# Split first units, paired slot sums, and two output rows computed ahead of the last sum, in a gated recurrence followed by a soft mixture of experts

## The chip, the cores and the metric

The kernel runs on one core of a Trainium2 chip. The core has five engines with a queue each: TensorE (PE, matmuls and transposes through matmul, results in PSUM), VectorE (DVE), ScalarE (ACT), GpSimd (POOL) and SyncE (SP, which here only issues DMAs). POOL issues the weight loads, and 16 DMA engines carry all transfers. The metric is device time in microseconds (us) of one execution; 0.5% of it is about 1 us.

## The reference

```python
# x, f_logit: (4, 5056, 256); phi: (256, 32); w1: (8, 256, 1024); w2: (8, 1024, 256)
sig = 1.0 / (1.0 + np.exp(-f_logit))
f = lower_bound + (1.0 - lower_bound) * sig
i = 1.0 - f
for t in range(S):
    h = f[:, t] * h + i[:, t] * x[:, t]
    y[:, t] = h
x = y.reshape(B * S, D)                      # 20224 tokens
logits = x @ phi                             # 32 slots, 4 per expert
d = softmax(logits over tokens)              # per slot
slot_input = d.T @ x                         # 32 x 256
slot_out[e] = relu(slot_input[e] @ w1[e]) @ w2[e]
c = softmax(logits over slots)               # per token
return c @ slot_out
```

A recurrence over 5056 tokens in four batches is followed by two softmaxes over the same logits: one over all tokens, which gathers 32 slot inputs, and one over the slots, which spreads the experts' results back over the tokens. No output row can be finished before all tokens have been read.

## The kernel before, in words

A unit is 512 tokens of one batch (`G = 128 * R`, `R = 4`); there are 10 groups of tokens (`n_grp`) and 4 batches, so 40 units (`n_unit`). `place(n)` says which group and batch unit n is. Two units with numbers 2m and 2m+1 share the tiles of a load. The order of the instructions on every engine is the order in which the program writes them (`manual_schedule`).

For a unit the steps are: `load` (SP issues the DMAs of `f_logit` and `x` into `f_t`, `x_t`, three buffers each); `gate` (ACT, line 234: `s_t` = sigmoid(-f), for two units at once, for one in units 0 to 3); `enter` (POOL, line 245: `u_t` = s * x; DVE for unit 0); `s_to_channels` and `u_to_channels` (PE transposes into PSUM tiles `sp`, `up`, lines 249, 257, 264: tokens on partitions become channels on partitions); `decay` (ACT, lines 297, 304: a = 1 - (1-lb) s); `scan` (DVE, lines 319, 332: the recurrence, two instructions per unit, carrying on from the previous group of the batch); `to_tokens` (PE, line 345: transposes back into `hp`) and `keep_tokens` (line 364: copy into `ht`, by ACT or DVE). After four units of a group: `logits` (PE, line 378), `exps` (ACT, line 387: exp into `etall`, which stays in SBUF for all tokens), `weights_to_tokens` (PE transposes, line 399, and a copy, line 402), and `slots` (PE, line 428), which adds exp(logits).T @ h of a group to one PSUM tile `slot_ps`, 32 rows per batch:

```python
for b in range(B):
    nc.tensor.matmul(slot_ps[ds(b * NS, NS), :], et[:n_p, r, b], ht[:n_p, b, r], ...)
```

`idle(k)` (line 183) issues fp32 matmuls that no result needs. `W_AT` says after which unit's `enter` POOL issues the next weight load (`load_w`); 16 loads of 512 KB in SBUF (1 MB in memory, cast on the way), the last one, the second matrix of expert 7, in chunks of 4, 2 and 2 of its 8 slices (line 147, into `w_sb` and `w_t`).

The loop over the units writes, in iteration n, the loads of unit n+6, the gate of n+3 or n+4, the enter of n+3, transposes of units n+1 to n+3, the scan of n, and copies and sums of earlier units. After it come the last group's sums, the copy of the slot sums to `slot_sb` (line 615), four matmuls that sum the batches into `sin_ps` (line 619, a corner of the tile `tail`, in which PE also writes row sums of `etall` at line 411), the scaling into `sin` (631, 632), the first expert matrices (line 648) with relu (653, 655), transposes (663), the second matrices of experts 0 to 3 (684) and of experts 4 to 7 (line 696, into `so_ps`, after which `spin` issues eight matmuls, line 152), the scaling by the reciprocal `rcs` of the softmax sum into `slot_out` (DVE, line 708), and two copies of it with rows of every other batch zeroed, `slot_bd` (POOL, line 710).

The output is then computed in blocks of rows: `share` (line 727) multiplies `etall` of 128 tokens by `slot_out` of a batch; `by_vector` (DVE, 717) and `by_scalar` (ACT, 721, 767) scale by `rrow`, the reciprocal of the row sums; SP issues the DMAs to memory. The first are `pieces(0, 0)`: block 0 (2048 tokens, 16 rows a partition) of batch 0 in five DMAs of 2, 2, 2, 4 and 6 rows (line 749); then `by_rows` of the last block, two batches at once through `slot_bd` (lines 760, 770); then `rest`, `whole` (789) and `couple` (801 to 815).

Of the kernel before, what the change touches and what calls it, by code (L numbers as in the profile page):

```python
# [18 lines left out]
def kernel(  # L19
# [62 lines left out]
    nc.vector.tensor_copy(ident, ident_f)  # L82

# [78 lines left out]
    with tc.tile_pool(name="sp2", bufs=3) as sp2, \  # L162
# [10 lines left out]
        slot_ps = slot_bank[:, 0]  # L173
# [3 lines left out]
        def idle(k, first=False):  # L177
            if first:
                for i in range(2):
                    nc.tensor.matmul(slot_bank[:, 1, ds(0, P)], ident, ident,  # L180
                                     start=True, stop=False, skip_group_check=True)
            for _ in range(k):
                nc.tensor.matmul(slot_bank[:, 1], ident_f, wide_rep,  # L183
                                 start=False, stop=False, skip_group_check=True)
# [75 lines left out]
        def half_to_channels(n, ps, t):  # L260
            k = ds(n % 2 * (P // 2), P // 2)
            v = ps.rearrange("c p r -> c (p r)").rearrange("c (p r) -> c p r", r=2 * R)
            for r in range(2 * R):
                nc.tensor.transpose(v[:, :, r], t(r)[k].bitcast(F32), ident_f[k, k])  # L264
# [10 lines left out]
        def u_to_channels(n):  # L275
            ps = psu.tile([P, P, R], F32, name="up", tag="up")
            if long(n):
                half_to_channels(n, ps, lambda r: uts[n - n % 2 + r // R][:, r % R])
# [143 lines left out]

        def slots(g):
            n_p = rows(g)
            et, ht = ets.pop(g), hts.pop(g)
            for r in range(R):
                for b in range(B):
                    nc.tensor.matmul(slot_ps[ds(b * NS, NS), :], et[:n_p, r, b],
                                     ht[:n_p, b, r],
                                     start=(g == 0 and r == 0),  # L430
                                     stop=(g == n_grp - 1 and r == R - 1),
                                     skip_group_check=True)
# [37 lines left out]
        def late_slots():  # L470
            for r in range(R):
                for b in range(B):
                    nc.tensor.matmul(slot_ps[ds(b * NS, NS), :], ets[last][:, r, b],
# [10 lines left out]
        lb_constants()  # L484
        gate(0, 1)
# [3 lines left out]
        u_to_channels(0)  # L489
        gate(1, 1)  # L490
# [3 lines left out]
        s_to_channels(1)  # L494
        u_to_channels(1)
# [3 lines left out]
        for n in range(n_unit):  # L499
            if n < SINGLE - 2:  # L500
# [7 lines left out]
                if n + 3 == SINGLE:  # L508
                    gate(n + 3)
                if n % 2 == 0:  # L510
                    unit(load, n + AHEAD)
                unit(enter, n + 3)
                for b in range(2 * n, 2 * n + 2):
                    rep_constants(b)
            else:
# [31 lines left out]
                if n == n_unit - 2:  # L547
                    keep_tokens(n - 1)
                if n % 2 == 0:
# [320 lines left out]
```

## Time and profile before

| what | value |
|---|---|
| time before, median of 3 runs | 197.21 us (196.96 to 197.81) |
| the profiled execution's own time | 197.01 us |
| its span, first to last instruction | 195.2 us |
| mean granted TensorE clock | 0.845 |
| busy: PE, DVE, ACT, POOL | 150.6, 142.0, 138.8, 103.1 us |
| moved by DMA | 70.75 MB; HBM read 58.23 MB, written 20.71 MB |

The page divides the span into 40 slices of 4.88 us and gives for each the busy share of an engine in tenths (9 is 90% or more), the clock that TensorE was granted and the busy share of the 16 DMA engines. The chain that ended last is followed back from the last instruction: at each step to what released it. A line of the timeline has the start, the length, the engine, the line of the kernel, the operation, the tiles written and read, the shape, the count, and in brackets how long the engine was idle before and what ended that. A line of the table of stretches has the stretch, its length, the busy time and number of instructions of each engine, the granted clock, the DMA share and GB/s. Loads of weights count in GB/s with what is written to SBUF, half of what is read, as they are cast.

### The profile page before, as it was taken

The numbers are of one execution on the slowest core, as the hardware profiler recorded it, in microseconds if no ns is written. First come the engines' busy times: TensorE is split into PE (matmuls) and PEld (weight loads), VectorE is DVE, ScalarE is ACT, GpSimd is POOL, SyncE is SP. The second block draws the span as 40 slices with busy tenths as digits, with TensorE's granted clock in tenths as the row PEclk, the third lists the DMA queues.
The fourth block names the chain that finished last, engine by engine and source line by source line (L and its number), as shares of the span: only waits on it lengthen the run. The fifth ranks groups of instructions, "written<-read, shape, count | busy, mean of one in ns | idle before, by whom it ended". The sixth has DMA issues, their size and how long they took to land.

```text
span 195.2 us, 3283 instructions
## 1 busy us (share of the span) xinstructions
PE 150.6 (77%) x1222; PEld 108.7 (56%) x1222; DVE 142.0 (73%) x175; ACT 138.8 (71%) x192; POOL 103.1 (53%) x78
## 2 busy tenths in 40 slices
PE   0684896898998979989798976999997999980000
PEld 0474775765786657857576755766872663420000
DVE  2666699799699999999999999824288867770000
ACT  3686778599988998989988698724068788991000
POOL 2584888756798949776888979592030000000000
PEclk9998799699699999999999999999985555555555
DMA  6999999999999999999999999999949999999995
GB/s 203 415 433 428 426 425 421 430 426 411 326 428 426 423 334 405 423 425 414 324 418 418 235 212 214 214 212 211 170 165 428 425 431 426 430 433 430 430 430 218
DMA packets 12145, 70.75 MB, mean 362 GB/s; under 512 B 1361, under 2 KB 1874, under 8 KB 7650
## 3 DMA queue, kind: packets, MB, share of 16 engines
q1 hardware_dynamic: 9504, 62.13, 76.3%
q0 software_dynamic: 2624, 8.42, 21.8%
q8 instruction: 9, 0.15, 0.3%
q14 instruction: 6, 0.05, 0.1%
q10 hardware_dynamic: 2, 0.00, 0.0%
HBM read 58.23 MB, written 20.71 MB: 404 GB/s over the span
## 4 chain that ended last, share of the span: by engine, by line
PE 36%; DVE 28%; DMA 17%; ACT 4%; issue 4%; SPq 1%; POOL 0%; ACTq 0%
DVE h L332 17%; DMA w_t<-in_moe_w_dram 7%; PE op L801 7%; PE sp L249 7%; PE op L727 6%; DMA w_sb<-in_moe_w_dram 6%; PE hp L345 5%; DVE ht L364 5%; PE up L264 4%; DMA f_t<-in_f_logit_dram 4%; DVE h L319 3%; DVE oc L717 2%; PE op L760 2%; ACT s_t L234 1%; PE lg L378 1%
## 5 line engine op out<-in xcount | busy, mean ns | idle before, releaser
L245 POOL TENSOR_TENSOR u_t<-s_t,x_t 128x1024 bf16<-128x1024 bf16 (+1 forms) x39 | 82.4, 2129 | 24.5 <-ACT s_t L234 14.2
L332 DVE TENSOR_TENSOR_SCAN h<-a,h,up 128x512 bf16<-128x512 f32 x64 | 78.1, 1267 | 9.0 <-PE up L264 4.3
L234 ACT ACTIVATE s_t<-f_t 128x2048 bf16<-128x2048 f32 (+2 forms) x22 | 38.1, 1736 | 2.9 <-DMA f_t<-in_f_logit_dram 2.9
L345 PE MATMUL hp<-ident_f,h 128*128 128x128 f32 (+1 forms) x160 | 29.3, 307 | 8.4 <-DVE ht L364 6.3
L297 ACT ACTIVATE a<-sp,lbs 128x1024 f32<-128x1024 bf16 x28 | 29.6, 1112 | 4.6 <-PE sp L249 4.5
L345 PEld LDWEIGHTS hp<-ident_f,h 128*128 128x128 f32 (+1 forms) x160 | 23.2, 206 | 17.0 <-DVE ht L364 11.5
L249 PE MATMUL sp<-ident_f,s_t 128*128 128x128 f32 x144 | 23.7, 315 | 7.0 <-ACT s_t L234 5.7
L249 PEld LDWEIGHTS sp<-ident_f,s_t 128*128 128x128 f32 x144 | 19.6, 164 | 8.7 <-ACT s_t L234 6.5
L264 PE MATMUL up<-ident_f,u_t 64*128 64x64 f32 x224 | 21.4, 236 | 2.4 <-POOL u_t L245 2.4
L264 PEld LDWEIGHTS up<-ident_f,u_t 64*128 64x128 f32 x224 | 17.0, 144 | 7.1 <-POOL u_t L245 2.8
L721 ACT ACTIVATE ob<-op,rrow 128x256 f32<-128x256 f32 x32 | 12.4, 478 | 9.1 <-PE op L727 8.7
L364 ACT COPY ht<-hp 128x512 f32<-128x512 f32 (+1 forms) x21 | 12.2, 583 | 7.9 <-PE hp L345 7.9
L304 ACT ACTIVATE a<-sp,lbs 128x512 f32<-128x512 bf16 (+2 forms) x16 | 13.2, 868 | 2.9 <-PE sp L249 2.7
L183 PE MATMUL slot_ps<-rep,ident_f 128*128 128x256 f32 x42 | 14.2, 426 | 0.0
L364 DVE COPY ht<-hp 128x512 f32<-128x512 f32 (+1 forms) x19 | 12.7, 668 | 1.0 <-PE hp L345 1.0
L801 PE MATMUL op<-slot_bd,etall 64*128 64x512 bf16 x32 | 13.1, 627 | 0.0
L812 ACT ACTIVATE oc<-op,rrow 128x256 f32<-128x256 f32 x32 | 12.2, 486 | 0.8 <-PE op L801 0.3
L727 PE MATMUL op<-slot_out,etall 32*128 32x256 bf16 x64 | 12.6, 375 | 0.1
L806 DVE TENSOR_TENSOR oc<-op,rrow 128x1024 f32<-128x1024 f32 x8 | 9.7, 1223 | 3.4 <-PE op L801 3.4
L717 DVE TENSOR_TENSOR ob<-op,rrow 128x1024 f32<-128x1024 f32 (+2 forms) x12 | 9.8, 862 | 2.2 <-DMA out_dram<-ob 1.1
L727 PEld LDWEIGHTS <-etall 32*128 32x128 bf16 x64 | 8.9, 153 | 3.8 <-issue 1.3
L378 PE MATMUL lg<-h,phi 128*32 128x512 bf16 (+1 forms) x80 | 9.9, 389 | 0.2 <-ACT et L402 0.2
(109 smaller groups left out, 168.9 us busy)
## 6 DMA issues: line engine op xcount, KB each, us to landing
f_t<-in_f_logit_dram SPq DMA_DIRECT2D x14, 1024.0 KB, 11.2
x_t<-in_x_dram SPq DMA_DIRECT2D x14, 1024.0 KB, 9.5
out_dram<-oc SPq DMA_DIRECT2D x4, 2048.0 KB, 13.1
w_sb<-in_moe_w_dram POOLq DMA_DIRECT2D x14, 512.0 KB, 9.5
out_dram<-ob SPq DMA_DIRECT2D x3, 2048.0 KB, 9.6
f_t<-in_f_logit_dram SPq DMA_DIRECT2D x8, 512.0 KB, 7.0
x_t<-in_x_dram SPq DMA_DIRECT2D x8, 512.0 KB, 6.1
out_dram<-oc SPq DMA_DIRECT2D x4, 896.0 KB, 6.0
```

The source lines that it names most:

```text
L183: nc.tensor.matmul(slot_bank[:, 1], ident_f, wide_rep, start=False, stop=False, skip_group_check=True)
L234: nc.scalar.activation(s_t, f_t, ACT.Sigmoid, scale=-1.0)
L245: nc.gpsimd.tensor_tensor(uts[n][:, :r], s_t[:, :r], x_t[:, :r], ALU.mult)
L249: nc.tensor.transpose(ps[:, :, r], t[:, r].bitcast(F32), ident_f)
L264: nc.tensor.transpose(v[:, :, r], t(r)[k].bitcast(F32), ident_f[k, k])
L297: nc.scalar.activation(a, sp[:, :, :, :, o], ACT.Identity, scale=nomlb[:, ds(o, 1)], bias=1.0)
L332: nc.vector.tensor_tensor_scan(h[:, :T, o], decays[n // 2, o][:, n % 2, :T], up[:, :T, o], hs[number(g - 1, b)][:, ds(used(g - 1) - 1, 1), ...
L345: nc.tensor.transpose(hp[:n_p, r], hw[:, :n_p, r], ident_f)
L364: copy(hts[g][:n_p, b].rearrange("p r d -> p (r d)").bitcast(F32), hps.pop(n)[:n_p].rearrange("p r c -> p (r c)"))
L717: nc.vector.tensor_tensor(ob, op, scale.broadcast_to(list(ob.shape)), ALU.mult)
L727: nc.tensor.matmul(op[:, j], ew[:, :, r + j], slot_out[ds(b * NS, NS)], start=True, stop=True, skip_group_check=True)
L801: nc.tensor.matmul(op[:, i_r].rearrange("p u d -> p (u d)"), ew[:, :, r + i_r], slot_bd[ds(j * 2 * NS, 2 * NS)].rearrange("s u d -> s (u d)"),
```

## The change

Three groups of edits.

In the first units, the gate of units 4 and 5 is issued as two instructions of one unit each; the enter of unit 4 is written ahead of two copies of `rep`; `idle` gets a new form (its stationary operand is the zeroed tile `left`, its result goes to 64 rows of the slot sums, which it leaves as they are) and is called in more places before unit 13.

The slot sums move to a tile with two column halves. For groups 0 to 5 a matmul takes two batches' weights (64 columns) and two batches' tokens (512 columns), of which two blocks of four are the sums that are wanted; later groups use one matmul per batch as before, in the half `b % 2`. The sums are copied out in four pieces of 32 rows by DVE and ACT, and `sin_ps` gets a PSUM tile of its own.

For the output, the last two slices (`LATE = 2`) of expert 7's second matrix are left out of `so_ps` and summed in `end_ps`. Batch 3 (`D3`) takes the place of batch 0 in `pieces`. For its first two rows the softmax weights of expert 7's four slots, times `rcs` (`own`, `near`), are multiplied by the hidden values of those two slices (`near_ps`, `mix`) before the last slices are there; when they arrive, `ops` is formed from `so_b` (what is known without them) and `mix` times the slices. `slot_out` is formed from `end_ps` and `so_f`. The spins are five of 512 columns and stand ahead of the last two experts. The pools `osb` and `pfirst` are opened with `reuse_waits="tile"`: their tiles wait for earlier users of their own bytes alone.

```diff
+    D3 = B - 1
+    own = consts.tile([P, 1], F32, name="own")
+    nc.vector.tensor_reduce(own, ident_f[:, ds(P - SPE, SPE)], AX.X, ALU.add)
...
-        def idle(k, first=False):
...
+        def idle(k, first=False, moving=wide_rep):
+            for i in range(k):
+                nc.tensor.matmul(slot_bank[ds(0, L), 0], zeros, moving,
+                                 start=first and i == 0, stop=False, skip_group_check=True)
...
+                if r == R and rests:
+                    idle(2)
                 nc.tensor.transpose(v[:, :, r], t(r)[k].bitcast(F32), ident_f[k, k])
...
+                half_to_channels(n, ps, lambda r: uts[n - n % 2 + r // R][:, r % R],
+                                 n == 3 * B)
...
+        def slot_of(b):
+            return slot_bank[ds(b * NS, NS), b % 2]
...
+                if g < PAIRED:
+                    for b in range(0, B, 2):
+                        nc.tensor.matmul(slot_bank[ds(b * NS, 2 * NS)],
+                                         et[:n_p, r, ds(b, 2)].rearrange("p b s -> p (b s)"),
+                                         ht[:n_p, ds(b, 2), r],
...
         lb_constants()
+        idle(3, True, plain)
...
         u_to_channels(0)
+        idle(2, moving=plain)
...
         s_to_channels(1)
+        idle(1, moving=plain)
...
                 if n + 3 == SINGLE:
-                    gate(n + 3)
+                    gate(n + 3, 1)
+                    gate(n + 4, 1)
                 if n % 2 == 0:
                     unit(load, n + AHEAD)
-                unit(enter, n + 3)
+                if n == 0:
+                    unit(enter, n + 3)
                 for b in range(2 * n, 2 * n + 2):
                     rep_constants(b)
+                if n:
+                    unit(enter, n + 3)
...
+                if n == SINGLE - 2:
+                    idle(4, moving=plain)
...
-                elif n == SINGLE - 2:
-                    idle(1, True)
+                elif n in (SINGLE - 2, SINGLE - 1, SINGLE + 1, SINGLE + 3):
+                    idle(1)
...
-        nc.vector.tensor_copy(slot_sb, slot_ps)
-        sin_ps = tail[:, 0, ds(G // 2, DC * NS)].rearrange("p (o s) -> p o s", o=DC)
+        for b in range(B):
+            copy = nc.scalar.copy if b % 2 else nc.vector.tensor_copy
+            copy(slot_sb[ds(b * NS, NS)], slot_of(b))
+        sin_ps = psu.tile([P, DC, NS], F32, name="sin_ps", tag="up")
...
+                nc.vector.tensor_tensor(own, own, rcs, ALU.mult)
+                nc.gpsimd.tensor_scalar_mul(
+                    near[k3], etall[k3, ds(0, P * wide_r)].rearrange(
+                        "s (p r) -> s r p", r=wide_r)[:, ds(0, 2)], own[k3])
...
+        for i in range(LATE):
+            nc.tensor.matmul(near_ps[:, i].rearrange("p r t -> p (r t)"),
+                             hi_v[k3, FC - LATE + i], near[k3].rearrange("s r t -> s (r t)"),
+                             start=True, stop=True, skip_group_check=True)
+        mix = ew.tile([P, LATE, 2, P], BF16, name="mix")
+        nc.scalar.copy(mix.rearrange("p f r t -> p (f r t)"),
+                       near_ps.rearrange("p f r t -> p (f r t)"))
-        spin(tail[:, 1], 8, P)
-        nc.vector.tensor_scalar_mul(slot_out, so_ps, rcs)
+        spin(tail[:, 1], 5, G)
+        experts(so_ps, 2, range(FC))
+        experts(so_ps, 3, range(FC - LATE), last=True)
+        so_f = ew.tile([P, D], F32, name="so_f")
+        so_b = ew.tile([P, D], BF16, name="so_b")
+        nc.scalar.activation(so_b[k3], so_ps[k3], ACT.Copy, scale=rcs[k3])
+        nc.vector.tensor_scalar_mul(so_f, so_ps, rcs)
+        end_ps = pm.tile([P, D], F32, name="end_ps", tag="pm")
+        experts(end_ps, 3, range(FC - LATE, FC), first=True, last=True)
+        ops = []
+        for r in range(2):
+            op = pbig.tile([P, H], F32, name="hi_ps", tag=f"hi_ps{r}")[:, ds(0, D)]
+            ew_r = etall[k3, ds(0, P * wide_r)].rearrange("s (p r) -> s p r", r=wide_r)
+            nc.tensor.matmul(op, ew_r[:, :, r], so_b[k3], start=True, stop=False,
+                             skip_group_check=True)
+            for i in range(LATE):
+                nc.tensor.matmul(op, mix[:, i, r], w2_sb[E - 1][:, FC - LATE + i],
+                                 start=False, stop=i == LATE - 1, skip_group_check=True)
+            ops.append(op)
+        nc.vector.scalar_tensor_tensor(slot_out, end_ps, rcs, so_f, ALU.mult, ALU.add)
...
-    with tc.tile_pool(name="osb", bufs=3) as osb:
+    with tc.tile_pool(name="osb", bufs=3, reuse_waits="tile") as osb:
...
-            r0 = 0
-            for k in (1, 1, 1, 2, 3):
+            for r in range(2):
+                (by_scalar, by_vector)[r](ob[:, ds(r, 1)], ops[r].unsqueeze(1),
+                                          scale_of(i, b, r, 1))
+            nc.sync.dma_start(out=dst[:, ds(0, 2)], in_=ob[:, ds(0, 2)])
+            r0 = 2
+            for k in (1, 1, 2, 3):
...
-            pieces(0, 0)
+            pieces(0, D3)
...
-        for b in range(1, B):
+        for b in range(D3):
             whole(0, b)
```

## The prediction

> **What bounds the kernel now.** I read the page's slices first, then the chain that ended last, then stretches of time with the DMA share, and the timeline around the last weight chunk.
>
> ```profile
> DMA  6999999999999999999999999999949999999995
> ...
> 115.00 11.64 DMA w_sb<-in_moe_w_dram
> ...
> 126.92 14.59 DMA w_t<-in_moe_w_dram
> 141.52 0.04 issue
> 141.56 0.39 PE so_ps L696 x2
> 141.95 0.02 issue
> 141.98 0.49 DVE slot_out L708
> ```
>
> The DMA engines are full from the third microsecond to the end, but for one hole in the slice from 141.5 on. The chain enters a transfer of weights at 115.00 and leaves it at 141.52: there the kernel waits for bytes and for no engine. What DVE did before (100% busy from 82 to 100 and from 107 to 126 in the table of stretches) isn't what ends last.
>
> ```profile
> 141.50:142.00 0.50, 0.44 (x7) 0.41 (x7) 0.02 (x1) 0.00 (x0) 0.00 (x0) 1.00 0.00 0
> ...
> 143.50:144.00 0.50, 0.50 (x7) 0.50 (x6) 0.50 (x3) 0.50 (x3) 0.50 (x2) 1.00 0.00 0
> 144.00:144.50 0.50, 0.48 (x5) 0.33 (x4) 0.50 (x2) 0.50 (x3) 0.47 (x1) 1.00 0.16 53
> 144.50:145.00 0.50, 0.48 (x2) 0.28 (x3) 0.50 (x2) 0.50 (x3) 0.00 (x0) 0.82 1.02 393
> ...
> 139.50 1.79 PE L696 MATMUL so_ps<-w_t,wide 128*128 128x256 bf16 x14
> ...
> 141.56 0.38 PE L696 MATMUL so_ps<-w_t,wide 128*128 128x256 bf16 x2 [0.27 <-DMA w_t<-in_moe_w_dram]
> ...
> 143.58 2.84 SPq L749 DMA_DIRECT2D out_dram<-ob  x5
> ```
>
> Columns of the first four: stretch, its length, busy time of PE, weight loads, DVE, ACT and POOL, granted clock, DMA share, GB/s. Nothing moves from 141.5 to 144.4: 2.9 us, the only time that can be won without fewer bytes. Output follows at some 426 GB/s to the end. PE waited only 0.27 us for the last chunk; its work before that has almost no room.
>
> **Part 1: shorter first units and idle matmuls.** Their effect is read at DVE, whose scans carry the recurrence.
>
> ```profile
> 16.56 1.91 ACT L234 ACTIVATE s_t<-f_t 128x2048 bf16<-128x2048 f32 x1
> ...
> 18.52 1.97 PE L249 MATMUL sp<-ident_f,s_t 128*128 128x128 f32 x8 [2.68 <-ACT s_t L234]
> ...
> 21.44 2.46 DVE L332 TENSOR_TENSOR_SCAN h<-a,h,up 128x512 bf16<-128x512 f32 x2 [2.63 <-PE up L249]
> ...
> 39.11 2.45 DVE L332 TENSOR_TENSOR_SCAN h<-a,h,up 128x512 bf16<-128x512 f32 x2 [1.51 <-PE up L264]
> ```
>
> The scan of unit 3 waits for transposes that stand behind those of units 4 and 5, which wait for one sigmoid of 1.91. Cut in two (1.06 each, as units 0 to 3 have it; ACT pays 2 x 1.06 - 1.91 = 0.21), the first half is out at 17.6, and the second's transposes start at 18.7. With PE warm, four take 0.63 instead of 1.0 (rows L345 at 15.20, L249 here), so the scan starts near 20.1: 1.3 earlier. POOL's product for unit 4 can't start before its x tile, issued at 5.61, lands 12.6 later at 18.22; it started at 18.60, so what it hands on is 0.4, and 0.7 more for unit 5, for which the two copies of `rep` (0.61) no longer stand between. I take 1.0 (0.4 to 1.3).
>
> Fifteen more idle matmuls of fp32, two records 0.214 apart each (as the fp32 rows of L700), are 6.4 us of PE warm, 12.8 cold, in places where PE waits for ACT, POOL or a transfer. The clock fell to half from 35.59 to 39.00 and from 49.24 to 52.66, and DVE lost 1.51 and 1.61 at their ends. Both stay away at best: 3.1 gained. At worst neither does, and the five that stand ahead of transposes in the loop cost 5 x 0.43 = 2.1. I take 2.0, nearer to the best, as the matmuls fill the very stretches ahead of the falls.
>
> **Part 2: slot sums in pairs.** Six groups change from 16 matmuls of 256 columns into 32 rows (0.62 a group) to 8 of 512 columns into 64 rows. Bounds: the logits row, 8 of 512 columns into 32 rows, takes 1.08; without any overlap 8 x 0.218 + 0.16 = 1.9. So +0.46 to +1.3 a group, and from below 0 if the halved number of instructions pays for it. I take 0.46, the row of the same length, x 6 = 2.8 on PE. PE lies on the chain where two groups are summed (53 to 54, 76, 99), so about half reaches DVE: 1.4 (0 to 4). Lead of the compute by 126: 1.0 + 2.0 - 1.4 = 1.6 us, from -4 to +4.4.
>
> None of this lead ends the kernel earlier: the last chunk lands at 141.52 because DMA has been full. It only pays for Part 3.
>
> **Part 3: between the scans and the last chunk.** Four copies of 32 rows, two each on DVE and ACT, for one of 0.42: 0.42 to 0.84, I take 0.8 as the columns are the same. Against that, the scaled slot input waited 1.49 for row sums in its own tile (DVE at 131.21); with a tile of its own it needs copies to 130.1, four matmuls (0.61) and 0.1: 130.9. Gain 0.3. `own`, `near` (POOL, 32 rows x 256, under the 0.92 of L710) and `mix` (ACT, like the 0.60 of L653) run on engines idle from 133 to 141: nothing; uncovered, 1.6 us.
>
> In PE's queue, two matmuls for `near_ps` (0.11 each) and five spins of 512 columns (0.22 each) now stand ahead of the last two experts: 1.3 us. Their 14 matmuls could end at 139.50 + 14 x 0.109 (start to start) = 141.03, so now at 142.33, less 0.3 from the slot input, less the lead. A lead of 0.5 brings that to 141.5, when the chunk lands; I have 1.6. What those 1.3 would cost uncovered is in the first rival.
>
> **Part 4: after the last chunk.** Before: two matmuls, 0.48 of DVE, a matmul, 0.48 of ACT, first issue 143.58. Now: two matmuls from 141.56, then three for row 0 and three for row 1, the last starting at 141.56 + 7 x 0.109 = 142.33. DVE has finished `slot_out` (141.98 to 142.47, as before: its input comes no later). A result is read 0.33 after its matmul starts, so row 1 is scaled on DVE from 142.66 to 143.09 and row 0 on ACT from 142.33 to 142.8. Issue at 143.16: 0.42 earlier. The next pieces: DVE 143.09, 143.50, 143.90; issues 143.58, 143.97, 144.67 against 144.03, 144.50, 145.01, never later than the transfer before them ends (0.61 for 256 KB). `reuse_waits="tile"` keeps the later pieces from waiting for rows 0 and 1; nothing is added on SP's queue, where five issues stay five.
>
> How much of 0.42 reaches the end? The 2 MB of pieces last 4.9 us, to 149.3 before, 148.9 now. The next transfer was issued at 148.21 and moves 0.8 later (143.58 to 144.4), at 149.0. Its rows hang on `slot_bd`, whose POOL products end at 144.47 as before, and on seven matmuls at half clock (0.427 apart). So DMA waits 0.1: the gain is 0.3 (0 to 0.45).
>
> **Sum.** The profiled execution took 197.01 (span 195.2, 1.8 around it), 0.20 under the median of three. 197.01 - 0.3 = 196.7; 196.9 from the median. I say 196.8. What a measurement of this kernel can tell from no change is about 0.5%, 1.0 us (its three runs lie 0.85 apart), so this is a forecast of "within".
>
> **Rivals.**
> *PE comes late.* If the lead is nil, the chunk is taken up at 142.33 - 0.3 = 142.03, 0.5 late; `slot_out` and `slot_bd` move with it: 197.21 + 0.5 - 0.25 (the room of the next transfer) = 197.5; each microsecond of negative lead adds one. For it: PE's 0.27. Against: DVE's waits above.
>
> *The clock falls before the last chunk (the other side).* With a lead PE runs dry after the spins and then has 14 matmuls, 1.5 us of work, in the 3 us until the last chunk. For it: the table of stretches.
>
> ```profile
> 45.83:49.24 3.41, 2.44 (x30) 1.00 1.03 390
> 49.24:52.66 3.42, 3.42 (x20) 0.50 1.04 304
> ...
> 141.40:144.82 3.42, 3.09 (x28) 1.00 0.11 43
> 144.82:148.23 3.41, 3.41 (x13) 0.50 1.06 425
> ```
>
> Here (PE busy, clock, DMA share, GB/s) the clock fell with PE busy 2.44 and even 3.09 of 3.41, the latter on matmuls of 32 rows. Falling some 3 us earlier, it makes the 14 matmuls of the pieces 0.21 apart: 1.5 later, so by_rows begins at about 146, its transfer comes 1.7 late; less 0.25 of room, 197.0 + 1.4 = 198.4. It decides when the lead is over about 2.5, as the spins then lie a whole stretch ahead. Against it: spins and 14 matmuls are 2.6 of work within some 4 us.
> The Trainium skill ("TensorE: Matmul & The Clock Gate", Part 1 and its table of goals) says that the clock halves after an idle window of about 3.4 us and that gaps over about 3 us are to be avoided. By that rule no gap here is long enough and the time would be 196.8; the rows, with falls after stretches without such a gap, leave the rival open.
>
> *The lead passes to the end*, if the loads and not DMA's rate set 141.52: 197.2 - 1.6 = 195.6 or less. Against it: DMA share 0.9 to 1.2 in every stretch from 3 to 140.
>
> *The gain is hidden anyway*: rows of the next transfer later by 0.3, and 197.1.
>
> **How the numbers follow.** Forecast 0.45 (196.4 to 197.0 as its own range), hidden 0.18, PE late 0.14, clock 0.16, lead to the end 0.07. Faster (under 196.2): 0.07, and 0.09 of the forecast's case with a clock that stays up longer: 0.16. Slower (over 198.2): 0.10 of the clock, 0.04 of PE late: 0.14. The rest, 0.70, is the same. The range 196.0 to 198.3 leaves out under 2 in 10.
>
> **What would show it.** Right: w_t landing at 141.5 again, scans ending 1 to 3 us before 125.6, PE idle before the last chunk, first output issue near 143.2, clock at full until then. Wrong: the last experts' matmuls back to back past 141.6; the clock row at half before 141; a last landing of weights that moved by over 0.5; DMA under 1.0 between 148 and 150 for longer than 0.3.

## The result, and the profile after

The kernel after took 201.83 us (median of 6 runs, 200.73 to 202.59) against 197.23 (196.96 to 197.81): ratio 1.0226 [1.0203, 1.0249]. It is slower by 4.6 us; I had forecast 196.8 and no change. In three kernels below one execution each (206.56, 201.17 and 201.23 us) fell into a slower state of the chip and is left out of the medians and ranges. The profiled execution took 202.34 us, its span 200.6, at a mean clock of 0.854 (before 195.2 and 0.845).

The slices of the page: the clock before, then clock and DMA share after:

```profile
PEclk9998799699699999999999999999985555555555
...
PEclk9999759999999999999999999999985555555555
DMA  5999999999999999999999999999429999999996
```

DMA is still marked full until the hole, but the hole has a second slice. The clock falls for the output no earlier than before; once it had come up, it was at half one time before that, from 22.59 to 29.41, and in before three times, the last two from 35.59 to 39.00 and from 49.24 to 52.66. Next the chain that ended last (start, length, what):

```profile
128.85 0.55 PE slot_ps L446 x16
129.40 0.35 PE tail L474 x4
129.74 0.55 PE slot_ps L446 x15
130.33 0.65 PE slot_ps L488 x16
131.00 0.42 DVE slot_sb L641
131.45 0.37 ACT slot_sb L641
131.84 0.43 DVE slot_sb L641
132.30 0.37 ACT slot_sb L641
...
132.72 0.66 PE sin_ps L645 x4
...
142.00 0.37 PE near_ps L744 x2
142.37 0.32 PE tail L156
...
143.55 1.54 PE so_ps L730 x14
145.12 0.47 ACT so_b L755
...
146.84 0.43 DVE ob L778
```

Before, the chain went through a transfer of weights from 115.00 to 141.52. Now no transfer of weights is in it: from the slot sums at 128.85 to the first output it is PE and the copies between PE's steps. The last experts' matmuls run back to back, one of the signs that I had named for "wrong". The timeline has the same place with the idle time before each instruction and what ended it:

```profile
143.39 1.69 PE L730 MATMUL so_ps<-w_t,wide 128*128 128x256 bf16 x14
144.91 0.38 PE L730 MATMUL end_ps<-w_t,wide 128*128 128x256 bf16 x2
145.12 0.47 ACT L755 ACTIVATE so_b<-so_ps,rcs 32x256 bf16<-32x256 f32 x1 [2.13 <-PE so_ps L730]
...
145.62 0.48 DVE L756 TENSOR_SCALAR so_f<-so_ps,rcs 128x256 f32<-128x256 f32 x1 [3.71 <-ACT so_b L755]
...
147.18 2.50 DVE L778 TENSOR_TENSOR ob<-op,rrow 128x256 f32<-128x256 f32 x5
...
147.33 0.35 SPq L804 DMA_DIRECT2D out_dram<-ob  x1
147.62 2.66 ACT L782 ACTIVATE ob<-op,rrow 128x256 f32<-128x256 f32 x7 [0.89 <-PE op L788]
```

The last weights landed at 144.31 (before 141.52), and yet PE didn't wait for them. Where the 5.35 us of the two profiled executions come from, in us:

| stretch | before | after | difference |
|---|---|---|---|
| to the end of the last scan (DVE) | 125.63 | 127.33 | +1.70 |
| from there to the scaling of the slot input, `sin` | 5.58 | 6.16 | +0.58 |
| from there to the first output issue | 12.37 | 13.84 | +1.47 |
| from there to the last output landing | 50.44 | 52.04 | +1.60 |

### The profile page after: what moved, and what is told of

It reads as the page before. It is cut to its first block, busy times and chain, and to the rows that moved or that the text cites. A ratio compares the mean times of both kernels' runs of the same rounds, so it can differ in the third digit from the quotient of the medians.

```text
span 200.6 us, 3262 instructions
## 1 busy us (share of the span) xinstructions
PE 160.3 (80%) x1204; PEld 105.8 (53%) x1205; DVE 143.7 (72%) x179; ACT 141.0 (70%) x197; POOL 104.2 (52%) x79
## 4 chain that ended last, share of the span: by engine, by line
PE 44%; DVE 18%; DMA 12%; ACT 8%; POOL 4%; issue 4%; SPq 1%; ACTq 0%; POOLq 0%; DVEq 0%
DVE h L337 11%; DMA x_t<-in_x_dram 9%; PE hp L350 7%; PE op L866 7%; PE sp L251 5%; PE up L268 5%; POOL u_t L247 4%; PE lg L383 3%; DMA out_dram<-ob 3%; PE slot_ps L185 3%; DVE ht L369 3%; PE slot_ps L439 2%; ACT s_t L236 2%; PE so_ps L730 2%; PE op L825 2%
## 5 line engine op out<-in xcount | busy, mean ns | idle before, releaser
L350 PE MATMUL hp<-ident_f,h 128*128 128x128 f32 (+1 forms) x160 | 29.8, 310 | 5.9 <-DVE ht L369 4.4
L350 PEld LDWEIGHTS hp<-ident_f,h 128*128 128x128 f32 (+1 forms) x160 | 22.2, 207 | 19.9 <-DVE ht L369 10.2
L251 PE MATMUL sp<-ident_f,s_t 128*128 128x128 f32 x144 | 20.5, 284 | 2.7 <-ACT a L309 1.4
L251 PEld LDWEIGHTS sp<-ident_f,s_t 128*128 128x128 f32 x144 | 16.9, 146 | 5.4 <-ACT s_t L236 3.1
L185 PE MATMUL slot_ps<-rep,left 128*64 128x256 f32 x52 | 16.5, 409 | 0.0
L337 DVE TENSOR_TENSOR_SCAN h<-a,up 128x512 bf16<-128x512 f32 x8 | 9.3, 1208 | 1.7 <-PE up L268 1.1
```

Of the source, the lines that this page charges most:

```text
L185: nc.tensor.matmul(slot_bank[ds(0, L), 0], zeros, moving, start=first and i == 0, stop=False, skip_group_check=True)
L251: nc.tensor.transpose(ps[:, :, r], t[:, r].bitcast(F32), ident_f)
L337: nc.vector.tensor_tensor_scan(h[:, :T, o], decays[n // 2, o][:, n % 2, :T], up[:, :T, o], hs[number(g - 1, b)][:, ds(used(g - 1) - 1, 1), ...
L350: nc.tensor.transpose(hp[:n_p, r], hw[:, :n_p, r], ident_f)
```

## The experiments

Every kernel here computes the whole reference. Where I give the landing of single packets, it is read from the trace's DMA records.

**The tiles back on multiples of 256 bytes.** The new tile `own` has 4 bytes, takes 32, and shifts all later tiles, so that load, weight and output tiles start 32 bytes behind a multiple of 256. First the kernel after with that undone, then the kernel before with the same shift.

```
-    PAD = 48
+    PAD = 32
```

> The whole change, with the padding behind the tile `etall` cut from 48 to 32 elements, so that every tile behind it lies at the address it had in the kernel before (multiples of 256 bytes; the new 4-byte tile `own` had moved all of them by 32 bytes). Theory A (the shift makes transfers slower: in the trace of the changed kernel an 8192-byte packet of the loads takes 313 to 320 ns where it took 309, and the last input lands 1.65 us later): packets of 309 ns again, inputs landed by 108.1 as before, time 201.8 - 2.6 = 199.2 us (1.65 of the loads, 0.4 of the weights, 0.6 of the output). Theory B (the rate differs by chip or by what PE reads from the same memory, not by address): packets stay at 313 to 320 and the time at 201.8.

```
-    PAD = 48
+    PAD = 64
```

> The kernel before, with the padding behind `etall` 64 elements instead of 48: every tile behind it moves by 32 bytes and nothing else changes. Theory A: packets of 313 to 320 ns, inputs landed 1.65 us later, time 197.2 + 2.6 = 199.8 us. Theory B: 197.2 us.

The first: 201.11 us (200.48 to 201.85), ratio to before 1.0198 [1.0161, 1.0235]. Its median is 0.7 less than after's, but the two ranges overlap. The second: 198.77 (198.64 to 198.94), 1.0079 [1.0056, 1.0102], 1.5 more than before and clear of its range. GB/s by slice, of before and of before with the shift:

```profile
GB/s 203 415 433 428 426 425 421 430 426 411 326 428 426 423 334 405 423 425 414 324 418 418 235 212 214 214 212 211 170 165 428 425 431 426 430 433 430 430 430 218
```

```profile
GB/s 200 411 423 423 416 418 419 421 423 390 334 428 423 403 330 426 421 420 362 370 413 405 258 214 214 214 213 213 161 151 415 419 418 429 423 429 429 439 426 230
```

In the first full slices 433, 428 and 426 became 423, 423 and 416. The 3584 load packets of 8192 bytes took 310.6 ns on average at multiples of 256 and 314.5 off them, the 896 output packets of 16384 bytes 611.5 and 617.1. So the shift costs time, but alone it is a third of the loss at most (1.5 of 4.6), and undoing it in the changed kernel gave back a sixth. I had expected 2.6 us from either. The Trainium skill ("DMA: Bandwidth & Descriptors", "How a descriptor splits into AXI transactions") says that the first transaction of a descriptor that doesn't start on 256 bytes begins at the boundary below, so that bytes are fetched for nothing; the direction agrees with the 1% by which packets are longer here. I had not looked at addresses at all.

**The front part alone, on before.**

Of the diff's hunks, all those on `idle`, `gate` and `enter`, and no other:

```
+        idle(3, True, plain)
...
-                    gate(n + 3)
+                    gate(n + 3, 1)
+                    gate(n + 4, 1)
```

> The kernel before with the first part of the change alone (two short gates for units 4 and 5, the order of POOL's work, the new idle matmuls in their new places), all tiles at their old addresses. If the compute's lead only makes PE wait longer for the weights: 197.2 us within 0.4, scans ending 1 us or more before 125.6. If the idle matmuls delay the scans (they ended later in the changed kernel, though its first scans were earlier): scans end after 125.6 and the time goes up by as much, less 0.3: 197.5 to 198.5 us.

It took 199.15 us (198.79 to 200.88), 1.0115 [1.0065, 1.0164], although its scans ended 1.04 earlier (124.59). Its timeline at the last weights:

```profile
139.14 1.03 PE L707 MATMUL so_ps<-w_t,wide 128*128 128x256 bf16 x8 [0.51 <-DMA w_t<-in_moe_w_dram]
...
141.39 0.95 PE L707 MATMUL so_ps<-w_t,wide 128*128 128x256 bf16 x6 [1.22 <-DMA w_t<-in_moe_w_dram]
...
142.56 0.38 PE L707 MATMUL so_ps<-w_t,wide 128*128 128x256 bf16 x2 [0.22 <-DMA w_t<-in_moe_w_dram]
```

The first chunk of the last load came 2.25 us after the load before it, not 1.31. No load was issued late. What was new at that moment is a packet of 16 KB on the page's "instruction" queue at 139.19, which takes 0.975 us. I take it for a fetch of PE's instructions, as the runs below move it by adding PE instructions. The page counts them:

```profile
q8 instruction: 10, 0.16, 0.3%
```

Before has 9, from the first to the eighth one per some 266 of PE's matmuls and weight loads; its last fell at 141.24, into the hole. Here the added matmuls move it to 139.19, among the last weights, and a tenth follows at 169.34. In the trace the landing of a DMA is told by 16 signals (the whole first load into `w_t` of before: from 137.70 to 138.92), as many as there are DMA engines; if a fetch sits on one engine, whoever needs all 16 waits. That is a correlation as yet; three runs test it.

**The number of PE instructions alone.** 28 one-column matmuls, in stretches where PE is idle:

```
+        def tiny(k):
+            for _ in range(k):
+                nc.tensor.matmul(slot_bank[:, 1, ds(0, 1)], ident, ident[:, ds(0, 1)], ...)
...
         lb_constants()
+        tiny(18)
...
         u_to_channels(0)
+        tiny(10)
```

> The kernel before with 28 one-column matmuls early on (18 after the constants, 10 after the first unit's transposes, both in idle stretches of PE), about as many PE instructions as the front part adds; nothing else changes. Theory F (a fetch of PE instructions, about 1 us on one of the 16 DMA rings once in some 256 PE instructions, holds up whatever transfer has to land on all 16): the fetch that lay in the hole between weights and output at 141.24 us moves to about 139 us, ahead of the last weight chunks, and one more falls into the output phase; last landing 142.5 us, time 198.2 to 199.2 us. Rival (the number of PE instructions is nothing, and the front part is slower by its idle matmuls or its gates): 197.2 us, within 0.3.

199.02 us, 1.0119 [1.0036, 1.0203]: as much as the front part costs, without the front part. Its profiled execution took 201.64, the other three 198.76 to 199.19, so its stages are not compared, only its output. That the other half of its cost lies ahead of the last weights is therefore not shown.

**The front part with 28 PE instructions fewer.**

```
+            pair = moving[:, ds(0, 1)].broadcast_to([P, 4, P])
-            for i in range(k):
-                nc.tensor.matmul(slot_bank[ds(0, L), 0], zeros, moving, ...)
+            for i in range(k // 2):
+                nc.tensor.matmul(slot_bank[ds(0, L)].rearrange("p u d -> p (u d)"), zeros, pair, ...)
```

> The front part alone (199.15 us), with its idle matmuls taken two at a time as one of 512 columns where there are two or more: the same time on PE, about 28 PE instructions fewer. Theory F: the fetch at 139.19 us goes back to about 141 to 142.5 us, into the hole, and the one in the output phase to its end or away; time 196.7 to 197.4 us. Rival (the idle matmuls or the gates themselves cost): 198.8 to 199.4 us, as the front part with single ones.

Profiled, the fetch went to 140.85 and the last weights landed at 141.53, 0.98 earlier than with single ones and as before: that half of the expectation held. But the tenth fetch only moved to 173.84, and the output phase stayed at 51.40. The profiled execution took 198.07 against 198.95; the median is 199.13 (197.85 to 200.69, 10 runs), 1.0095 [1.0058, 1.0132], so the medians show no gain. Nor does a fetch among the last weights always delay them: in four kernels below it lay at 140.95 to 141.18, and the last chunk landed at 141.45 to 141.74; in a fifth, with a fetch at 140.99, it landed at 143.00. A loss of about 1 us ahead of the first chunk is seen in the front part's trace alone.

**The kernel after, aligned, with 32 PE instructions more.**

```
         lb_constants()
+        tiny(8)
...
         u_to_channels(0)
+        tiny(8)
```

> The kernel after with its tiles back on multiples of 256 bytes (201.11 us), and 16 one-column matmuls early on, some 32 PE instructions more. Theory F: the fetch that lay on the first output pieces at 148.5 us moves ahead to 145 to 147 us, between the last landing and the first output; first issue to last landing goes from 51.4 to about 50.5 us, time 200.0 to 200.4 us. Rival (the slow start of the output comes from the output part's own waits): 201.1 us, within 0.4.

200.19 us (199.56 to 200.85), 0.9 less than aligned alone, with ranges that overlap a little (1.0149 [1.0093, 1.0205] to before): more instructions, less time. The fetch at 148.47 that had lain on the first output pieces went to 142.42, and the output phase from 51.39 to 50.64: the first output DMA landed 2.00 us after its issue, and 3.73 with the fetch on it. The rest of the difference of the two profiled executions (201.85 and 199.65) is that the scans of the second ended 1.47 earlier, which a fetch in the output can't explain.

First output issue to last landing, in all kernels (those below included), by what lay in it:

| kernels | us | in the output phase |
|---|---|---|
| before; paired sums with 50 tiny matmuls | 50.44; 50.42 | no fetch |
| output part; own first; after with tiny; no pairs, own first | 50.69; 50.67; 50.64; 50.64 | no fetch |
| aligned after; front; tiny; front wide; paired sums | 51.39; 51.39; 51.39; 51.40; 51.44 | a fetch at 148.47; 169.34; 172.04; 173.84; 157.10 |
| before with the shift | 50.83 | no fetch, tiles off 256 |
| after | 52.04 | a fetch at 148.40, tiles off 256 |
| no pairs; the same without spins | 52.05; 51.39 | no fetch, but an early fall of the clock (below) |

Like with like, a fetch in it costs 0.75 to 1.0 us wherever it lies. In the front part 95% of the 16 KB output packets had landed 48.07 us after the first issue (before: 48.03), the last at 51.02 (49.96); only three of the 2592 output packets landed later than before's last. That fits one engine that is behind while the others aren't. The Trainium skill ("Runtime: NRT & Kernel Launch", "Instruction fetch mechanics") has blocks of 16 KiB, 256 instructions, through a queue of their own, and calls their cost mostly hidden. Size and count about agree; the cost wasn't hidden for a fetch in the output phase.

**The paired slot sums alone, on before**, with their four copies, `sin_ps` in a tile of its own and the new form of `idle`, whose old form wrote into the second column half; then with 50 tiny matmuls, which give back the 100 PE instructions that the pairs save.

```
-                for b in range(B):
-                    nc.tensor.matmul(slot_ps[ds(b * NS, NS), :], et[:n_p, r, b], ...
+                if g < PAIRED:
+                    for b in range(0, B, 2):
+                        nc.tensor.matmul(slot_bank[ds(b * NS, 2 * NS)], ...
```

> The kernel before with the second part alone: slot sums in pairs for groups 0 to 5, the sums copied out in four pieces, a PSUM tile of its own for the slot input; tiles at their old addresses. In the changed kernel the four copies ran one after the other (0.41, 0.36, 0.42, 0.36 us, 1.67 in all against 0.42), and two groups' sums took 0.98 us each on the chain. Theory C (PE's weight stage becomes late by these): scaled slot input 1.2 us and more later than at 131.21, last experts taken up after the last chunk has landed, 197.2 + 0.9 = 198.1 us. Rival (there is room before the chunk): 197.2 us within 0.4.

> The paired slot sums alone (200.18 us), with 50 one-column matmuls early on, which give back the 100 PE instructions that the pairs took away; the computation is the same. Theory F and the chain: the fetches fall where the kernel before has them, the last one into the hole, none into the output phase, which goes from 51.44 back to 50.4 to 50.8 us; the last weights still land late, by the 1.0 us by which the pairs make the chain late; time 198.0 to 198.6 us. Rival (all 2.95 us are the pairs' lateness on the chain): 199.8 to 200.4 us.

Alone 199.94 us (199.89 to 200.43), 1.0149 [1.0111, 1.0186]; with the tiny matmuls 199.54 (198.46 to 199.96), 1.0106 [1.0055, 1.0158], more than I expected of it and less than the rival did. In the profiles the fetch accounts for 1.0 of the output phase (51.44 to 50.42); the medians differ by 0.4 only. The chain of the second, whose profiled execution is its fastest:

```profile
130.00 0.65 PE slot_ps L484 x16
130.65 0.02 issue
130.68 0.42 DVE slot_sb L633
131.10 0.02 issue
131.12 0.37 ACT slot_sb L633
...
140.76 2.66 PE so_ps L714 x24
143.42 0.02 issue
143.44 0.49 DVE slot_out L726
```

Without any of the output part PE is already last: 24 matmuls back to back until 143.42. The end of the last scan over all kernels (the tiny matmuls' outlying execution left out) is:

| | without pairs | with pairs |
|---|---|---|
| without front | 125.63, 124.74, 123.52, 125.24: mean 124.8 | 126.56, 127.00: mean 126.8 |
| with front | 124.59, 125.55, 123.51, 124.52, 124.73: mean 124.6 | 127.33, 127.49, 126.02: mean 126.9 |

The means differ by 2.0 and 2.4 with pairs and by 0.2 with the front part. But they mix the price of a part with what the clock did in the first 51 us: the scan that ends at 51.2 in before ends 0.75 earlier in the output part's kernel and 0.75 later in the same with own first, and neither has a change in that stage. So I compare scan by scan behind it. DVE's rows at two places, before and then after (windows 76.5 to 81 and 100 to 104, DVE alone):

```profile
78.36 3.83 DVE L332 TENSOR_TENSOR_SCAN h<-a,h,up 128x512 bf16<-128x512 f32 x3 [0.39 <-PE up L264]
...
101.07 3.64 DVE L332 TENSOR_TENSOR_SCAN h<-a,h,up 128x512 bf16<-128x512 f32 x3 [0.38 <-PE up L264]
...
79.06 2.46 DVE L337 TENSOR_TENSOR_SCAN h<-a,h,up 128x512 bf16<-128x512 f32 x2 [0.93 <-PE up L268]
...
102.45 2.45 DVE L337 TENSOR_TENSOR_SCAN h<-a,h,up 128x512 bf16<-128x512 f32 x2 [0.92 <-PE up L268]
```

At each of the two places all five kernels with pairs lose 0.53 to 0.55 against before, and the other nine nothing (within 0.02). Near 57 they lose 0.18 more than the kernels with the front part and no pairs. That makes 1.26 for the pairs. Another 0.15 to 0.18 is lost at each of four places (near 59, 82, 104 and 125) by every kernel with the new form of `idle`, with or without pairs, and by no other: 0.6 in all. Near 82 the four transposes behind an idle matmul take 0.75 us with the new form and 0.63 with the old.

**The output part alone, on before, aligned** (the hunks from `own` on that are neither front nor slot sums)**; then with the matmuls of the premultiplied weights ahead of those on the last chunk.**

```
-        experts(end_ps, 3, range(FC - LATE, FC), first=True, last=True)
         ops = []
         for r in range(2):
...
             nc.tensor.matmul(op, ew_r[:, :, r], so_b[k3], start=True, stop=False, ...)
+            ops.append(op)
+        experts(end_ps, 3, range(FC - LATE, FC), first=True, last=True)
+        for r, op in enumerate(ops):
             for i in range(LATE):
                 nc.tensor.matmul(op, mix[:, i, r], w2_sb[E - 1][:, FC - LATE + i], ...)
-            ops.append(op)
```

> The kernel before with the output part alone, its tiles on multiples of 256 bytes; no front part, no paired sums. My prediction: first issue 0.42 us earlier, time 196.8 to 197.0 us. Rival 1 (splitting the last experts and making the first two rows puts work behind the last landing that was not there): the stretch from the last landing to the first issue grows from 2.06 to 2.6 us or more, time 197.6 to 198.2 us. Theory F adds about 1 us to either if the last fetch leaves the hole.

> The output part alone (197.90 us; profiled 197.32, 2.13 us from the last landing to the first issue), with the two matmuls of the premultiplied weights and so_b moved ahead of the two matmuls on the last chunk, so that behind the landing all matmuls have 128 rows. Theory M (my step of 0.42 us failed only because matmuls of 32 rows between matmuls of 128 rows start 0.2 to 0.26 us after one another instead of 0.109): landing to first issue 1.6 to 1.7 us, time 0.3 to 0.4 us under the output part's, 196.9 us in a profile like that one. Rival (DVE's and ACT's evictions set the first issue): 2.0 to 2.1 us again, time unchanged.

The first: 197.90 us (197.26 to 199.01), 1.0050 [1.0022, 1.0078]. Its timeline behind the last landing at 141.48:

```profile
141.36 0.47 ACT L733 ACTIVATE so_b<-so_ps,rcs 32x256 bf16<-32x256 f32 x1 [2.84 <-PE so_ps L708]
...
141.52 0.39 PE L708 MATMUL end_ps<-w_t,wide 128*128 128x256 bf16 x2 [0.26 <-DMA w_t<-in_moe_w_dram]
...
141.88 0.29 PE L741 MATMUL hi_ps<-so_b,etall 32*128 32x256 bf16 x1
...
142.11 0.39 PE L744 MATMUL hi_ps<-w_t,mix 128*128 128x256 bf16 x2
...
142.43 0.33 PE L741 MATMUL hi_ps<-so_b,etall 32*128 32x256 bf16 x1
...
142.69 0.39 PE L744 MATMUL hi_ps<-w_t,mix 128*128 128x256 bf16 x2
...
143.61 0.35 SPq L782 DMA_DIRECT2D out_dram<-ob  x1
```

The first issue is at 143.61, before at 143.58: my 0.42 is not there. From a matmul of 32 rows to one of 128 and back the starts lie 0.20 to 0.26 apart, not 0.109. The Trainium skill ("TensorEngine Tiling (Array Packing)", "Key Properties") says that a change of the tiling mode drains TensorE; these rows agree. The second kernel took 198.24 (1.0048 [1.0022, 1.0073]), no better: in its profile PE was late (last scan 125.24, `so_ps` done at 142.33, landing 141.45), so its first issue, 144.60, is no test. It still shows the matmuls of 128 rows 0.11 apart, and that PE waited 0.61 for `so_b` ahead of them. Whether the slower executions of the first are such late ones isn't shown, as I have no profile of one.

**The kernel after without pairs; the same with own first; and that without the five spins.** Slot sums and their copy as before, idle matmuls joined, tiles aligned:

```
-        for b in range(B):
-            copy = nc.scalar.copy if b % 2 else nc.vector.tensor_copy
-            copy(slot_sb[ds(b * NS, NS)], slot_of(b))
-        sin_ps = psu.tile([P, DC, NS], F32, name="sin_ps", tag="up")
+        nc.vector.tensor_copy(slot_sb, slot_ps)
+        sin_ps = tail[:, 0, ds(G // 2, DC * NS)].rearrange("p (o s) -> p o s", o=DC)
```

and in the third kernel also

```
-        spin(tail[:, 1], 5, G)
```

> The kernel after without the paired slot sums: front part (idle matmuls joined to 512 columns, the two within the halved transposes left out, some 20 PE instructions fewer) and output part, tiles on multiples of 256 bytes. Theory P (the paired sums and their four copies make the compute chain late, and that alone sets after's first issue at 147.33 us): slot input scaled at about 131 us or before, last experts not back to back past the landing at 141.5 us, first issue 143.5 to 143.8 us, no fetch in the output phase, which takes 50.4 to 50.8 us; time 196.9 to 197.6 us. Rival (near, mix and the spins make PE late also without pairs): first issue 144.5 us or later, time 198.2 us or more.

> As the kernel without pairs, with the two matmuls of the premultiplied weights moved ahead of those on the last chunk. If theories M and P both hold: first issue 143.1 to 143.3 us, time 196.5 to 197.1 us, the fastest of all. If P falls: 198 us or more, whatever M does.

> The kernel without pairs, with the premultiplied weights' matmuls ahead of those on the last chunk (198.09 us; profiled 197.53: experts done at 142.94 us, 1.2 us behind the landing at 141.74), without the five 512-column matmuls that stand ahead of the last two experts in PE's queue and compute nothing (1.19 us there). Theory L (what is left is that PE comes late by those 1.2 us): so_ps done before the landing, landing to first issue 1.6 to 1.7 us (theory M), time 0.5 us less than the kernel with them, 196.9 to 197.4 us. Rival (they keep PE's clock, my rival of the clock that falls early): the clock falls to half before the last chunk, landing to first issue 2.5 us or more, 198 us or more.

They took 199.27 us (197.68 to 200.45; 1.0103 [1.0059, 1.0146]), 198.08 (197.53 to 199.53; 1.0052 [1.0022, 1.0083]) and 197.75 (197.32 to 200.02; 1.0032 [0.9999, 1.0065]), against 200.19 with pairs; each is above what I had expected of it. In two of the first's six executions (199.97 and 199.69) some 2.8 us lie outside the span, where it is 1.7 to 2.1 in the others; its spans have a median of 197.0. `sin` was scaled at 129.09, 130.10 and 130.31, with pairs at 132.18 and after at 133.49. The chain left PE and went back to the weights in the first and the third. Between the second and the kernel with pairs and tiny matmuls that is 2.08, of which the pairs' 1.26 and their copies' 0.58 are 1.84. So the pairs are what made the chain late in like kernels, but none of the three beats before. The second's `so_ps` was done at 141.63, ahead of the landing at 141.74, and still the first issue was 143.91 and not 143.1 to 143.3.

The first's profiled execution is its slowest, 200.45, and shows two mishaps: its last chunk came 1.97 us after the one before it (0.55 to 0.72 elsewhere), beside a fetch at 140.99 (which the others had without such a delay), and the clock fell at 145.20, just as the output began. From 145.10 on (stretch, length, busy times of PE, weight loads, DVE, ACT and POOL, clock, DMA share, GB/s), DMA was a third idle:

```profile
145.10:148.10 3.00, 2.98 (x14) 2.07 (x14) 2.32 (x5) 2.01 (x5) 0.86 (x1) 0.52 0.66 255
```

In the third kernel PE was in time, as its timeline shows; chunks landed at 140.94 and 141.62:

```profile
141.46 0.47 ACT L749 ACTIVATE so_b<-so_ps,rcs 32x256 bf16<-32x256 f32 x1 [1.71 <-PE so_ps L725]
...
141.97 0.38 PE L756 MATMUL hi_ps<-so_b,etall 32*128 32x256 bf16 x2 [0.61 <-ACT so_b L749]
...
142.28 0.39 PE L725 MATMUL end_ps<-w_t,wide 128*128 128x256 bf16 x2
...
142.51 0.60 PE L762 MATMUL hi_ps<-w_t,mix 128*128 128x256 bf16 x4
...
143.63 0.35 SPq L799 DMA_DIRECT2D out_dram<-ob  x1
```

Now the matmuls are 0.11 apart, but PE waited 0.61 for `so_b`, which comes from the chunk before the last; the first issue is again at 143.63. Both orders lose the 0.42, each to something that I had counted as free. This kernel's clock was at half from 144.41, 0.8 after its first issue: the 13 matmuls of the pieces took 2.21 us instead of 1.57, and the output phase 51.39 with no fetch in it. Against the 50.64 of the second kernel this is the price of the early fall, which my rival had put at 1.4: 0.75 here and 1.4 in the first kernel.

## Why the prediction was wrong

The forecast failed at "lead of the compute 1.6 us": in the trace of after the last scan ends 1.70 later than before's. The term of it that failed is the idle matmuls' 2.0; the pairs' 1.4 came out near its size. The rival "PE comes late" is what happened, far beyond the half microsecond that I gave it. Point by point:

- **What bounds the kernel.** "The last chunk lands at 141.52 because DMA has been full" was right for a lead: the output part's kernel issued the first late load at 103.35 and not 105.46, and its weights landed at 141.48. It was wrong for a lag: with a first late issue at 106.26 to 107.18 (the two kernels of pairs, after, after aligned) they landed at 142.91 to 144.84. I took "no gain from a lead" for "no loss from a lag". A full DMA share didn't say that bytes set the landing: in the paired kernel it is 1.02 to 1.07 in every 5 us from 100 to 140, and yet from 110 to 115 it moved 185 GB/s where before moved 205. PE's wait of 0.27, which I quoted, was the whole room on that side.
- **Part 1, +3.0.** The scan of unit 3 started at 19.63 instead of 21.44, more than my 1.3. The idle matmuls' 2.0 is the term that failed. After has neither of the two falls that I wanted away, but its clock was at half from 22.59 to 29.41, where before's was full from 21.93 on: a scan that ended 1.81 earlier (23.9 in before) was followed by one 1.87 later (34.7) and, as before then had its fall at 35.59, by one 0.75 later (51.2). Without the fall at 49.24 it won 0.92 back, and it lost 0.6 by the new form of `idle`, which I had at nothing. Part 1 came out at some -0.4. The 0.92 isn't the matmuls' doing either: the output part's kernel has no added idle matmul and no fall at 49.24. Other kernels with the front part lie between 1.82 ahead and 0.90 behind at 51.2. Why the falls move is not settled.
- **Part 2, -1.4.** A group's eight matmuls took 1.05 instead of 0.62, so +0.43, and I had said 0.46. "About half reaches DVE" was right: 1.26 of 2.6 (0.18, 0.54 and 0.54, each 2 to 4 us behind one of the three sums that I had named). So the lag of 1.70 is 0.75 less 0.92, plus 0.6 and 1.26.
- **Part 3, +0.3.** The copies took 1.67, not 0.8 and outside my bounds of 0.42 to 0.84: each waited for the one before it on the other engine (the chain above). All four read one tile in PSUM and write one tile in SBUF. The timeline of after speaks for the one that is read: `so_f` on DVE waits for `so_b` on ACT, though the two write different tiles and only read the same ones (`so_ps`, `rcs`), while both engines write `ob` side by side from 147.62 on, out of different `op` tiles. The tile of its own for `sin_ps` did save the wait for row sums. Net -0.58, not +0.3.
- **The 1.3 us of `near_ps` and spins** were 1.55 in the chain of after (0.37 and 1.18), and as PE was last there they cost all of it.
- **Part 4, +0.3.** Nothing: 2.13 us from landing to issue instead of 2.06, by the change between 32 and 128 rows, or by `so_b`. I had also let DVE finish `slot_out` at 142.47 "as before"; as `so_f` had to wait for `so_b`, it ran from 142.46 to 142.95 in the output part's kernel. In after itself, behind PE's late end, 2.24 us passed from the end of `so_ps` to the issue.
- **The rival's own arithmetic** gives 197.5 at no lead, 1.7 for the lag, 0.88 for `sin` late by 0.58 instead of early by 0.3: 200.1. The kernel after with alignment and fetch mended took 200.19. In part that is luck: the lag in its own trace is 0.39, for which the same arithmetic gives 198.8, and that execution took 199.65.
- **Missing altogether**: the 32 bytes of `own` and the place of a fetch. They are 0.7 and 0.9 as steps between medians of overlapping ranges (201.83, 201.11, 200.19), so they close the sum by construction; in the output phases of the profiles they are 0.65 and 0.75.
- **The parts don't add up.** Each alone on before costs something (front 1.9, pairs 2.7, output part 0.8, shift 1.5: 6.9), and the whole 4.6, so their costs are not independent.
- **The clock** stayed up from 29.41 until 148.88 in after, as forecast for the last chunk; the early fall is real in two other kernels.

Left open: why the executions of one changed kernel lie up to 3 us apart where before's mostly lie within 1 (a fetch near the last chunk, a clock that falls 1 us earlier, and PE within 0.4 of being late would each do it), why the clock falls where it does, and which DMA engine a fetch falls on.

## What to carry to other kernels

A transfer that ends last hides a lead, but not a lag: before counting on one, see how far the next bound lies behind, here 0.27 us. Don't count a fall of the clock in one trace as time to be won: two kernels that were alike in that stage ended the same scan 1.5 us apart, with the falls at other times. Price a changed loop by the same scan in both traces, not by its last one. Give a new small tile a place, or a pad, that leaves the large tiles' addresses alone. When a change adds or takes out some ten TensorE instructions, look where the page's instruction packets fall in the trace, and try a few instructions more or less before judging the change itself.

## What I had not expected of the hardware

- Adding 28 matmuls of one column cost 1.9 us (197.1 to 199.0), and adding 16 to another kernel gained 0.9. Half of the first (0.95) and most of the second (0.75) is the place of a 16 KB fetch in the output phase, which takes some 0.95 us where nothing else is in its way.
- 32 bytes of shift cost 1.5 us of 197 (packets of 8 KB 310.6 to 314.5 ns on average).
- Matmuls that alternate between 32 and 128 rows start 0.20 to 0.26 us apart, instead of 0.109.
- Two engines' copies out of disjoint rows of one PSUM tile ran one after the other, 1.67 us instead of 0.42 for one copy of all rows. Whether the chip or the order that the program asks for does it, no run here tells.
- Idle matmuls with a stationary operand of 64 columns instead of 128 (the new form of `idle`) cost the scans 0.15 us at each of four places.
